# Joining half-unit VectorE products, four Horner halves and a new step order in a sketched-attention and rational-MLP kernel

## The chip, the cores and the metric

The kernel runs on one core of a Trainium2 chip. The metric is the device time of one execution in microseconds (us); the time of a kernel is the median of several executions. The engines are named as in the profile: PE (TensorE, matmuls; PEld is its weight load), DVE (VectorE), ACT (ScalarE), POOL (GpSimd) and SP, whose queue issues nearly all DMAs.

## The reference

```python
def phi(x):                                   # q, k: (4, 4, 1088, 32); S1, S2: (8, 32)
    a = einsum('rd,bhsd->bhsr', S1, x); b = einsum('rd,bhsd->bhsr', S2, x)
    return einsum('bhsi,bhsj->bhsij', a, b).reshape(..., 64)
q_p, k_p = phi(q), phi(k)
kv  = einsum('bhsf,bhsd->bhfd', k_p, v);  z = k_p.sum(axis=2)
x   = einsum('bhsf,bhfd->bhsd', q_p, kv) / (einsum('bhsf,bhf->bhs', q_p, z)[..., None] + 1e-6)
x   = x.transpose(0, 2, 1, 3).reshape(4352, 128)
h   = x @ w_in                                # (4352, 2048)
P   = a0 + a1*h + a2*h*h + a3*h*h*h
Q   = 1 + |b0|*|h| + |b1|*h*h
out = (P / (Q + 1e-6)) @ w_out                # (4352, 128), float32
```

## The kernel before

The first half is a linear attention on sketched features. Keys and values of each of the four batches are loaded whole (`load_k`, `load_v`), transposed on DVE (`kt`), sketched by PE (`ks`, L262), copied by ACT (`kc`), multiplied into 64 features on DVE (`kf`, L274) and summed into kv and z on PE (`kp`, L303); ACT keeps the result (`kk`). Queries go in 13 blocks. For a block, DVE transposes (`qt`, L326), PE sketches (`qs`), ACT copies (`qc`), DVE multiplies (`qf`), PE makes numerator and denominator (`qp`, L366), DVE and ACT divide (`qd`, `qi`, `qx`), PE transposes back (`qb`, L392) and ACT stores the columns in `xT` (`qk`, L399). From block 3 on (class `Spread`), `qc` writes the sketches to DRAM with four DMAs (L421), and three more DMAs read them back with rows repeated, into `a_all` and `b_all` (L424, L427); L433 multiplies these. Each of these tiles has one buffer.

The second half is the MLP, in 17 units. A unit is 4096 columns: so many tokens (256, 512 or, at the end, twice 256) by so many blocks of 128 hidden features. For unit i, PE makes h in four parts of 1024 columns (`h0` to `h3`, L456, in two PSUM tiles `h_ps`), ACT evacuates each as bf16 into `hh` (`e0` to `e3`, L462). DVE computes Q - 1 as (|b1||h| + |b0|)|h| in `u`, `w`, `y` (L485, L491, L496), in one instruction of 4096 columns, or in two halves for the units in `SPLIT_A`. ACT computes r = 1/Q as exp(-ln Q) by halves of 2048 columns (`ln`, L547, and `ex`, L551). The sum a0 r + a1 h r + h h r (a2 + a3 h) is left to PE: `w_out` is held three times, plain and scaled by a0 and by a1. p = a3 h + a2 is made by ACT or DVE (`pa`, L542, or `pd`, L537, by the table `P_ON_ACT`, one entry for each half unit). s = h r is `s` (L555), g = h s is `m` (L559), then g = g p is `x` (L570). `G0` to `G5` (L589) are the matmuls: the blocks of r, s and g of the first half, then of the second.

A Horner half (table `HORNER`, by half unit) goes another way: m makes g = h p, `v` (L565) adds a1, x makes g = g s, and the matmuls on s are left out. So such a half has one DVE instruction more and four or eight matmuls less.

The steps s, m, x and p of a unit are two instructions of 2048 columns, or a single one of 4096 if the unit stands in `WIDE_S`, `WIDE_M`, `WIDE_X`, `WIDE_P` and its halves are of the same kind (both Horner or neither, for m and x; both on the same engine, for p). The tiles r, s and g are rings of four halves, p is a ring of two. Unit 16 is done in a half and two quarters.

The order is written out by hand: `ORDER` is a list of `step:index`, and each engine executes its instructions in that order. Loads are steps too: `lk`, `lv`, `lq` for a batch's keys, values and queries, `lx` for a half of `w_in`, `lw` for a half of `w_out` (cast by `wo`). They all stand in SP's queue with the sketches' DMAs and the stores of the results (`st`, L606, after a DVE transpose, L598). `tn` is a step of idle matmuls on PE (`TURNS`).

```python
    def skip(wide=(), same=None):
        def wrap(f):
            def step(i, h):
                if i in wide and i not in QUARTER and (same is None or same(i, 0) == same(i, 1)):
                    if h != 1:
                        return
                    h = "both"
```

Of the kernel before, what the change touches and what calls it, by code (L numbers as in the profile page):

```python
# [20 lines left out]
ORDER = """
tn:4 tn:0 lw:1 lq:0 kt0:0 lw:0 kt1:0 lx:1 kt2:0 lx:0 ks1:0 kt3:0 ks0:0 lk:1 qt:0 ks2:0 kc0:0 kc1:0 kf0:0 kf1:0 qs:0
kc2:0 qt:1 kf2:0 qc:0 kp0:0 ba:0 kp1:0 qf:0 kp2:0 wo:3 qs:1 kk:0 lv:1 qt:2 qp:0 qc:1 wo:1 qf:1 qs:2 qd:0 qi:0 qc:2
qp:1 qx:0 qf:2 wo:0 qb:0 qp:2 qd:1 qi:1 qk:0 qx:1 qt:3 h3:0 qd:2 qi:2 lq:1 qx:2 wo:4 wo:2 h2:0 e3:0 kt1:1 h0:0 kt0:1
e2:0 pa1:0 u1:0 lk:2 qs:3 w1:0 qb:2 h1:0 y1:0 qc:3 qk:2 e0:0 qt:5 qb:1 ks0:1 qt:4 e1:0 qs:4 qk:1 u0:0 ln1:0 h1:1 qt:6
w0:0 y0:0 kc0:1 ex1:0 h2:1 kf0:1 ks1:1 e1:1 s1:0 e2:1 h0:1 m1:0 kc1:1 ln0:0 kf1:1 h3:1 lq:2 e0:1 x1:0 e3:1 h1:2 kt0:2
ex0:0 u1:1 h2:2 qf:3 w1:1 qc:4 e1:2 qp:3 e2:2 s0:0 pa0:0 h3:2 y1:1 h0:2 qd:3 wo:5 e3:2 qi:3 m0:0 G0:0 e0:2 qx:3 G1:0
ln0:1 kt1:2 x0:0 qb:3 ks0:2 u1:2 qk:3 G2:0 ex0:1 lk:3 pd0:1 G3:0 w1:2 G4:0 pa1:1 kp1:1 y1:2 kc0:2 ln1:1 G5:0 qf:4 lv:2
qs:5 kf0:2 kk:1 ex1:1 qp:4 s0:1 ks1:2 qd:4 qc:5 qi:4 ln0:2 qt:7 G0:1 qx:4 m0:1 qb:4 G1:1 qk:4 s1:1 ex0:2 h3:3 x0:1
kc1:2 h2:3 m1:1 e3:3 kf1:2 h0:3 e2:3 kt1:3 ln1:2 s0:2 h1:3 st:0 m0:2 e0:3 qs:7 x1:1 e1:3 h2:4 ex1:2 u1:3 h3:4 pd1:2  # L30
pa0:2 w1:3 kp1:2 s1:2 e2:4 x0:2 e3:4 h0:4 lv:3 qf:5 pa0:3 y1:3 qp:5 qc:7 e0:4 h1:4 m1:2 qd:5 ln0:3 qi:5 qt:9 G2:1 qx:5
e1:4 x1:2 qb:5 G3:1 qk:5 u1:4 ex0:3 G4:1 m0:3 G5:1 pa1:3 G0:2 w1:4 h0:5 kt0:3 ln1:3 m1:3 h2:5 y1:4 kk:2 ex1:3 ks0:3
G1:2 e0:5 s1:3 G2:2 ln0:4 G3:2 h1:5 v0:3 ex0:4 qf:7 x0:3 G4:2 e2:5 qs:6 s0:4 qc:6 h3:5 e1:5 pd0:4 ln1:4 m0:4 h1:6 v1:3
e3:5 x0:4 pa1:4 h0:6 u1:5 qt:8 G5:2 e1:6 w1:5 ex1:4 h3:6 st:2 y1:5 e0:6 qp:7 e3:6 s1:4 G0:3 pa0:5 lq:3 G2:3 x1:3 qs:8
m1:4 h2:6 ln0:5 m0:5 G3:3 e2:6 x1:4 G5:3 ex0:5 qf:6 G0:4 u1:6 G1:4 qc:8 qd:7 ln1:5 qi:7 qp:6 w1:6 G2:4 qx:7 qd:6 pa0:6
qi:6 v0:5 qb:7 G3:4 qx:6 y1:6 qb:6 qk:7 G4:4 qk:6 ex1:5 h3:7 m0:6 pa1:5 G5:4 s1:5 h1:7 e3:7 st:4 h2:7 m1:5 e1:7 ln0:6
x0:5 h0:7 qt:10 x1:5 e2:7 G0:5 e0:7 qf:8 ks1:3 kc0:3 ex0:6 u1:7 qs:9 h1:8 v0:6 qc:9 w1:7 ln1:6 h3:8 s0:6 e1:8 pd1:6
qp:8 ex1:6 y1:7 h0:8 e3:8 s1:6 kc1:3 ln0:7 h2:8 x0:6 e0:8 m1:6 G2:5 qd:8 ex0:7 G3:5 qi:8 kf0:3 G4:5 kf1:3 G5:5 e2:8
qs:10 ln1:7 u1:8 kp1:3 qx:8 w1:8 ex1:7 qb:8 G0:6 qf:9 qk:8 y1:8 qc:10 h3:9 pa0:7 s0:7 h0:9 e3:9 s1:7 ln0:8 h2:9 qt:12
m0:7 e0:9 G0:7 x1:6 e2:9 h1:10 ex0:8 x0:7 qt:11 h1:9 u1:9 pa0:8 m1:7 G2:6 pd1:7 e1:9 G3:6 s0:8 e1:10 G4:6 u0:9 ln1:8  # L40
h3:10 w1:9 m0:8 qp:9 ex1:8 x1:7 h2:10 x0:8 qd:9 kk:3 e3:10 qi:9 w0:9 pa0:9 h0:10 qf:10 y0:9 qp:10 e2:10 y1:9 e0:10
G5:6 qx:9 qd:10 ln0:9 qi:10 qb:9 s1:8 G1:7 qx:10 G2:7 qk:9 u1:10 ex0:9 G3:7 m1:8 qb:10 G4:7 qk:10 s0:9 ln1:9 G5:7
qs:11 pd1:8 h1:11 w1:10 qc:11 ex1:9 x1:8 h0:11 e1:11 m0:9 pa1:9 h3:11 y1:10 e0:11 G0:8 s1:9 e3:11 h2:11 ln0:10 x0:9
h0:12 m1:9 e2:11 pd0:10 ex0:10 h1:12 u1:11 x1:9 e0:12 G1:8 w1:11 e1:12 G2:8 ln1:10 G3:8 s0:10 G4:8 y1:11 G5:8 ex1:10
qs:12 G0:9 m0:10 G1:9 ln0:11 h3:12 s1:10 ex0:11 x0:10 h2:12 qf:11 pa1:10 m1:10 G2:9 s0:11 G3:9 e3:12 G4:9 x1:10 qc:12
ln1:11 qp:11 pd0:11 m0:11 G5:9 qd:11 e2:12 G0:10 qi:11 x0:11 ex1:11 G1:10 u1:12 G2:10 pa1:11 qx:11 G3:10 w1:12 qb:11
G4:10 qk:11 s1:11 pa0:12 h1:13 y1:12 h3:13 e1:13 m1:11 ln0:12 h2:13 st:6 x1:11 ex0:12 G5:10 qf:12 G0:11 st:8 e3:13
qp:12 s0:12 e2:13 st:10 h0:13 ln1:12 m0:12 u1:13 h2:14 e0:13 x0:12 ex1:12 u0:13 h3:14 w1:13 w0:13 e2:14 y1:13 e3:14
h1:14 pa1:12 y0:13 h0:14 s1:12 qd:12 e1:14 qi:12 m1:12 G1:11 e0:14 qx:12 G2:11 ln1:13 u1:14 qb:12 G3:11 pd0:13 G4:11
ex1:13 w1:14 G5:11 x1:12 G0:12 qk:12 ln0:13 h0:15 s1:13 pd1:13 ex0:13 G1:12 y1:14 G2:12 e0:15 h2:15 s0:13 ln0:14 m1:13  # L50
h3:15 e2:15 m0:13 ex0:14 h1:15 x1:13 x0:13 e3:15 G3:12 s0:14 e1:15 h2:16 ln1:14 u1:15 G4:12 m0:14 ex1:14 G5:12 w1:15
G0:13 h3:16 pa0:14 st:12 y1:15 G1:13 e2:16 G2:13 s1:14 e3:16 h1:16 ln0:15 u2:16 u3:16 w2:16 w3:16 h0:16 x0:14 ex0:15
y2:16 G3:13 pd0:15 e0:16 G4:13 s0:15 e1:16 G5:13 y3:16 pa1:14 G0:15 u0:16 m0:15 G1:15 ln1:15 G0:14 m1:14 G1:14 w0:16
G2:14 ex1:15 x0:15 G3:14 y0:16 G2:15 v1:14 G3:15 ln0:16 s1:15 x1:14 ex0:16 pd1:15 G5:14 m1:15 G0:16 ln2:16 s0:16 G4:15
pa0:16 x1:15 G1:16 ex2:16 m0:16 G5:15 ln3:16 s2:16 x0:16 ex3:16 m2:16 G2:16 pa2:16 st:15 s3:16 G3:16 pa3:16 G4:16
st:14 x2:16 m3:16 G5:16 G6:16 x3:16 G7:16 G8:16 st:16
# [12 lines left out]
@with_exitstack  # L69
def kernel(  # L70
    ctx: ExitStack,
# [409 lines left out]

    @halves(SPLIT_A)
    def d_abs(i, c):
        t = mine(i, "u", mid, 1)
        nc.vector.tensor_scalar(out=t[:, c].bitcast(U16), in0=live[i]["hh"][:, c].bitcast(U16), scalar1=0x7FFF,  # L485
                                scalar2=None, op0=AX.bitwise_and)

    @halves(SPLIT_A)
    def d_w(i, c):
        t = mine(i, "w", mid, 2)  # L490
        nc.vector.tensor_scalar(out=t[:, c], in0=live[i]["u"][:, c], scalar1=ab1, scalar2=ab0, op0=AX.mult, op1=AX.add)  # L491

    @halves(SPLIT_A)
    def d_y(i, c):
        t = live[i]["w"]
        nc.vector.tensor_mul(out=t[:, c], in0=t[:, c], in1=live[i]["u"][:, c])  # L496
# [36 lines left out]

    @skip(WIDE_P, on_act)
    def d_p(i, h, hh):
        if not on_act(i, first(h)):
            nc.vector.tensor_scalar(out=part_of(i, "p", h), in0=hh, scalar1=a3, scalar2=a2, op0=AX.mult, op1=AX.add)  # L537

    @skip(WIDE_P, on_act)
    def a_p(i, h, hh):  # L540
        if on_act(i, first(h)):
            nc.scalar.activation(out=part_of(i, "p", h), in_=hh, func=ACT.Identity, scale=a3_reg, bias=a2)  # L542
# [9 lines left out]

    @skip(WIDE_S)
    def d_s(i, h, hh):
        nc.vector.tensor_mul(out=part_of(i, "s", h), in0=hh, in1=part_of(i, "r", h))  # L555

    @skip(WIDE_M, horner)
    def d_hs(i, h, hh):
        nc.vector.tensor_mul(out=part_of(i, "g", h), in0=hh, in1=part_of(i, "p" if horner(i, first(h)) else "s", h))  # L559
# [6 lines left out]

    @skip(WIDE_X, horner)
    def d_g(i, h, hh):
        g = part_of(i, "g", h)
        nc.vector.tensor_mul(out=g, in0=g, in1=part_of(i, "s" if horner(i, first(h)) else "p", h))  # L570
# [149 lines left out]
```

## Time and profile before

| what | us |
|---|---|
| median of 3 executions (271.52 to 271.73) | 271.63 |
| the profiled execution | 272.05 |
| its span, first to last instruction | 270.3 |
| L456 on PE, 320 records | 125.3 |
| L462 on ACT, 68 | 67.6 |
| L547 and L551 on ACT, 35 each | 66.0 and 65.7 |
| L542 on ACT, 23 | 44.5 |
| L555, L559, L570 on DVE, 33, 30 and 30 in their largest group | 41.1, 35.3, 35.1 |
| L496, L491, L485 on DVE, 22 each | 39.4, 23.8, 21.3 |

The busy times of a line are sums of durations of its records; an f32 matmul has two records. The records of DVE and ACT overlap a little where one instruction follows another at once, so the sum over lines is more than the busy time of an engine. A stretch of the span is read from a table by windows, and single instructions from rows in order of time, which hold start, duration, engine, line, output and inputs.

### The profile page before, as it was taken

To read this page: it belongs to the slowest core of one execution; us is meant where nothing else is said; L and a number is where in the kernel's file an instruction comes from. 1 tells how busy PE (TensorE), PEld (TensorE's weight loads), DVE (VectorE), ACT (ScalarE), POOL (GpSimd) and SP (SyncE) were. 2 spreads that over 40 slices of the span, in tenths; PEclk is the share of its full clock that TensorE was granted. 3 is DMA by queue.
4 is the path that set the end of the run, shared out by engine and by line. 5 is a ranking of instruction groups with operands and counts; after the bars stand their busy time and mean duration, and the time that the engine had idled before them with its cause. 6 is when DMAs were issued, how large, how long until landed. Compare 5 with 4: busy or idle time off the path is not lost.

```text
span 270.3 us, 3749 instructions
## 1 busy us (share of the span) xinstructions
PE 257.8 (95%) x1397; PEld 147.5 (55%) x1397; DVE 256.2 (95%) x278; ACT 247.2 (91%) x224; POOL 2.9 (1%) x24
## 2 busy tenths in 40 slices
...
GB/s 165 281 309 152 148 43 125 124 85 109 63 119 37 12 114 104 76 76 33 97 6 121 9 0 4 118 11 0 18 93 73 44 0 0 2 39 1 0 2 79
DMA packets 30530, 19.55 MB, mean 72 GB/s; under 512 B 20400, under 2 KB 26672, under 8 KB 30512
## 3 DMA queue, kind: packets, MB, share of 16 engines
...
q10 hardware_dynamic: 1648, 0.40, 0.7%
q8 instruction: 11, 0.18, 0.3%
q14 instruction: 7, 0.06, 0.1%
...
## 4 chain that ended last, share of the span: by engine, by line
PE 44%; ACT 25%; DVE 15%; issue 7%; DMA 6%; SPq 1%; DVEq 0%; ACTq 0%
PE h_ps L456 21%; PE att_ps L589 17%; ACT hh L462 8%; ACT ln L547 8%; ACT r L551 6%; DVE s L555 3%; DMA w_in_sb<-in_moe_w_in_dram 3%; DVE w L496 3%; ACT p L542 3%; PE att_ps L366 2%; DVE g L559 2%; DMA q_sb<-in_q_dram 2%; DVE g L570 1%; DVE w L491 1%; DVE k_p L274 1%
## 5 line engine op out<-in xcount | busy, mean ns | idle before, releaser
L456 PE MATMUL h_ps<-xT,w_in_sb 128*128 128x512 f32 (+1 forms) x320 | 125.3, 536 | 2.9 <-ACT hh L462 1.9
L456 PEld LDWEIGHTS h_ps<-xT,w_in_sb 128*128 128x128 f32 x320 | 58.4, 190 | 54.6 <-issue 37.2
L462 ACT CAST hh<-h_ps 128x1024 bf16<-128x1024 f32 x68 | 67.6, 1026 | 4.5 <-PE h_ps L456 4.2
L589 PEld LDWEIGHTS <-w_out 128*128 128x128 bf16 x460 | 45.6, 100 | 45.8 <-issue 14.1
L547 ACT ACTIVATE ln<-w 128x2048 f32<-128x2048 bf16 (+1 forms) x35 | 66.0, 1886 | 0.8 <-DVE w L496 0.7
L551 ACT ACTIVATE r<-ln 128x2048 bf16<-128x2048 f32 (+1 forms) x35 | 65.7, 1878 | 0.6
L542 ACT ACTIVATE p<-hh,a_sb 128x2048 bf16<-128x2048 bf16 (+1 forms) x23 | 44.5, 1940 | 0.2 <-DVE g L570 0.2
L555 DVE TENSOR_TENSOR s<-hh,r 128x2048 bf16<-128x2048 bf16 (+2 forms) x33 | 41.1, 1248 | 0.0
L496 DVE TENSOR_TENSOR w<-w,u 128x4096 bf16<-128x4096 bf16 (+2 forms) x22 | 39.4, 1800 | 0.1
L589 PE MATMUL att_ps<-g,w_out 128*128 128x512 bf16 (+1 forms) x160 | 35.9, 353 | 3.7 <-DVE g L570 3.7
L589 PE MATMUL att_ps<-r,w_out 128*128 128x512 bf16 (+1 forms) x160 | 36.0, 355 | 0.0
L559 DVE TENSOR_TENSOR g<-hh,s 128x2048 bf16<-128x2048 bf16 (+1 forms) x30 | 35.3, 1178 | 0.0
L570 DVE TENSOR_TENSOR g<-g,p 128x2048 bf16<-128x2048 bf16 (+1 forms) x30 | 35.1, 1180 | 0.1
L589 PE MATMUL att_ps<-s,w_out 128*128 128x512 bf16 (+1 forms) x140 | 29.9, 343 | 0.0
L491 DVE TENSOR_SCALAR w<-u,b_abs 128x4096 bf16<-128x4096 bf16 (+2 forms) x22 | 23.8, 1092 | 0.0
L485 DVE TENSOR_SCALAR u<-hh 128x4096 uint16<-128x4096 uint16 (+2 forms) x22 | 21.3, 973 | 0.0
L366 PEld LDWEIGHTS att_ps<-kvz,q_pT 128*128 128x128 f32 x144 | 17.7, 191 | 4.7 <-issue 2.0
L366 PE MATMUL att_ps<-kvz,q_pT 128*128 128x66 f32 x144 | 17.9, 273 | 0.2 <-ACT kvz L315 0.2
L537 DVE TENSOR_SCALAR p<-hh,a_sb 128x2048 bf16<-128x2048 bf16 x12 | 9.7, 810 | 0.0
L303 PEld LDWEIGHTS att_ps<-v_sb,k_p 128*64 128x64 f32 (+1 forms) x288 | 8.8, 138 | 1.7 <-DVE p L537 0.8
L303 PE MATMUL att_ps<-v_sb,k_p 128*64 128x64 f32 (+1 forms) x288 | 9.2, 223 | 0.2 <-DMA v_sb<-in_v_dram 0.2
L255 DVE STREAM_TRANSPOSE kT<-k_sb 128x224 f32<-128x224 f32 (+4 forms) x10 | 5.9, 617 | 3.7 <-DMA k_sb<-in_k_dram 3.7
...
## 6 DMA issues: line engine op xcount, KB each, us to landing
...
```

Source lines behind the costliest of these rows:

```text
L366: nc.tensor.matmul(self.nd[:, o:o + 2 * KW], lhsT=self.q_p[:, c, x:x + 128], rhs=kvz[self.b % 2][:, c, :], start=True, stop=True)
L456: nc.tensor.matmul(t[:, x * tl:(x + 1) * tl], lhsT=w_in_sb[:, f * 128:(f + 1) * 128], rhs=xT[:, x_at(t0):x_at(t0) + tl], start=True, stop= ...
L462: nc.scalar.copy(out=live[i]["hh"][:, part * PW:(part + 1) * PW], in_=live[i]["h", part])
L491: nc.vector.tensor_scalar(out=t[:, c], in0=live[i]["u"][:, c], scalar1=ab1, scalar2=ab0, op0=AX.mult, op1=AX.add)
L496: nc.vector.tensor_mul(out=t[:, c], in0=t[:, c], in1=live[i]["u"][:, c])
L542: nc.scalar.activation(out=part_of(i, "p", h), in_=hh, func=ACT.Identity, scale=a3_reg, bias=a2)
L547: nc.scalar.activation(out=t, in_=live[i]["w"][:, span(h)], func=ACT.Ln, bias=1.0 + 1e-6)
L551: nc.scalar.activation(out=part_of(i, "r", h), in_=live[i]["ln"], func=ACT.Exp, scale=-1.0)
L555: nc.vector.tensor_mul(out=part_of(i, "s", h), in0=hh, in1=part_of(i, "r", h))
L559: nc.vector.tensor_mul(out=part_of(i, "g", h), in0=hh, in1=part_of(i, "p" if horner(i, first(h)) else "s", h))
L570: nc.vector.tensor_mul(out=g, in0=g, in1=part_of(i, "s" if horner(i, first(h)) else "p", h))
L589: nc.tensor.matmul(outs[t0][:, :tl], lhsT=w_sb[y][:, f0 + x, :], rhs=part_of(i, key, h)[:, c:c + tl], start=done[0] == 0, stop=done[0] == ...
```

## The change

Tables and order change, no other code:

- `WIDE_S` goes from 2 units to 15, `WIDE_M` and `WIDE_X` to the same 12, `WIDE_P` from one unit to 8; these steps become one instruction of 4096 columns where the halves are of the same kind.
- `HORNER` has four halves (of units 0, 2, 6 and 9) in place of five (of units 3, 3, 5, 6 and 14).
- `P_ON_ACT` is assigned anew, 23 halves of 34 in place of 22.
- `SPLIT_A` has three units (0, 2, 16) in place of four (0, 9, 13, 16).
- `ORDER` is another order of all steps. At the start, `lx:1` is the first load behind the values, then `lq:0`, `lw:1`, `lk:1`, `lq:1`, `lx:0`, `lw:0`; before, it was `lw:1`, `lq:0`, `lw:0`, `lx:1`, `lx:0`, `lk:1`, `lv:1`, `lq:1`. Two idle matmuls (`tn:4`) go from the beginning to behind the first key sketches. Later loads and blocks have new places too.

```diff
@@ ORDER, from the beginning; all of its lines differ
-tn:4 tn:0 lw:1 lq:0 kt0:0 lw:0 kt1:0 lx:1 kt2:0 lx:0 ks1:0 kt3:0 ks0:0 lk:1 qt:0 ks2:0 kc0:0 kc1:0 kf0:0 kf1:0 qs:0
-kc2:0 qt:1 kf2:0 qc:0 kp0:0 ba:0 kp1:0 qf:0 kp2:0 wo:3 qs:1 kk:0 lv:1 qt:2 qp:0 qc:1 wo:1 qf:1 qs:2 qd:0 qi:0 qc:2
-qp:1 qx:0 qf:2 wo:0 qb:0 qp:2 qd:1 qi:1 qk:0 qx:1 qt:3 h3:0 qd:2 qi:2 lq:1 qx:2 wo:4 wo:2 h2:0 e3:0 kt1:1 h0:0 kt0:1
...
+tn:0 kt0:0 kt1:0 kt3:0 ks1:0 kt2:0 ks0:0 kc0:0 kc1:0 tn:4 qt:0 lx:1 ks2:0 qs:0 lq:0 kf0:0 ba:0 kp0:0 kc2:0 kf1:0 qt:1
+kp1:0 kf2:0 qc:0 qs:1 qf:0 qc:1 qt:2 kp2:0 qt:3 qs:2 qf:1 kk:0 qp:0 qc:2 qf:2 qp:1 qd:0 qs:3 qi:0 qx:0 qb:0 qk:0 qp:2
+qd:2 qd:1 lw:1 h3:0 lk:1 qi:2 qi:1 kt0:1 lq:1 wo:3 h2:0 qx:2 wo:5 qb:2 qt:4 wo:1 qx:1 qt:5 lx:0 qb:1 qs:4 kt1:1 lw:0
...
-P_ON_ACT = (1, 1, 0, 1, 1, 0, 1, 1, 0, 1, 1, 1, 1, 0, 1, 0, 1, 0, 1, 1, 0, 1, 0, 1, 1, 1, 0, 0, 1, 1, 0, 0, 1, 1)
-SPLIT_A = (0, 9, 13, 16)
+P_ON_ACT = (0, 1, 1, 1, 1, 1, 1, 1, 1, 1, 1, 0, 1, 1, 0, 0, 1, 1, 1, 0, 0, 1, 0, 0, 0, 1, 0, 1, 0, 1, 1, 1, 1, 1)
+SPLIT_A = (0, 2, 16)
...
-WIDE_S = (3, 5)
-WIDE_M = (5,)
-WIDE_X = (5, 14)
-WIDE_P = (2,)
-HORNER = (6, 7, 10, 12, 29)
+WIDE_S = (1, 2, 3, 4, 5, 6, 7, 8, 9, 10, 11, 12, 13, 14, 15)
+WIDE_M = (1, 3, 4, 5, 7, 8, 10, 11, 12, 13, 14, 15)
+WIDE_X = (1, 3, 4, 5, 7, 8, 10, 11, 12, 13, 14, 15)
+WIDE_P = (2, 3, 4, 6, 7, 8, 11, 15)
+HORNER = (0, 4, 13, 18)
```

More of the change, by code (lines that the diff above doesn't have):

```diff
@@ L21 @@
 ORDER = """
-tn:4 tn:0 lw:1 lq:0 kt0:0 lw:0 kt1:0 lx:1 kt2:0 lx:0 ks1:0 kt3:0 ks0:0 lk:1 qt:0 ks2:0 kc0:0 kc1:0 kf0:0 kf1:0 qs:0
-kc2:0 qt:1 kf2:0 qc:0 kp0:0 ba:0 kp1:0 qf:0 kp2:0 wo:3 qs:1 kk:0 lv:1 qt:2 qp:0 qc:1 wo:1 qf:1 qs:2 qd:0 qi:0 qc:2
-qp:1 qx:0 qf:2 wo:0 qb:0 qp:2 qd:1 qi:1 qk:0 qx:1 qt:3 h3:0 qd:2 qi:2 lq:1 qx:2 wo:4 wo:2 h2:0 e3:0 kt1:1 h0:0 kt0:1
-e2:0 pa1:0 u1:0 lk:2 qs:3 w1:0 qb:2 h1:0 y1:0 qc:3 qk:2 e0:0 qt:5 qb:1 ks0:1 qt:4 e1:0 qs:4 qk:1 u0:0 ln1:0 h1:1 qt:6
-w0:0 y0:0 kc0:1 ex1:0 h2:1 kf0:1 ks1:1 e1:1 s1:0 e2:1 h0:1 m1:0 kc1:1 ln0:0 kf1:1 h3:1 lq:2 e0:1 x1:0 e3:1 h1:2 kt0:2
@@ L27 @@
[L27 to L56, printed above, removed]
+tn:0 kt0:0 kt1:0 kt3:0 ks1:0 kt2:0 ks0:0 kc0:0 kc1:0 tn:4 qt:0 lx:1 ks2:0 qs:0 lq:0 kf0:0 ba:0 kp0:0 kc2:0 kf1:0 qt:1
@@ new lines @@
+kp1:0 kf2:0 qc:0 qs:1 qf:0 qc:1 qt:2 kp2:0 qt:3 qs:2 qf:1 kk:0 qp:0 qc:2 qf:2 qp:1 qd:0 qs:3 qi:0 qx:0 qb:0 qk:0 qp:2
+qd:2 qd:1 lw:1 h3:0 lk:1 qi:2 qi:1 kt0:1 lq:1 wo:3 h2:0 qx:2 wo:5 qb:2 qt:4 wo:1 qx:1 qt:5 lx:0 qb:1 qs:4 kt1:1 lw:0
+e3:0 qc:3 e2:0 pa1:0 u1:0 qk:2 h0:0 w1:0 e0:0 y1:0 h1:0 ks1:1 qk:1 e1:0 ln1:0 qt:6 ex1:0 h2:1 wo:4 wo:2 pd0:0 u0:0
+w0:0 m0:0 ks0:1 e2:1 kc1:1 h3:1 qs:5 y0:0 s1:0 kc0:1 h0:1 qf:3 kf1:1 lk:2 lv:1 kf0:1 e3:1 ln0:0 kt1:2 h1:1 qp:3 e0:1
+v0:0 qc:4 wo:0 m1:0 e1:1 h1:2 qd:3 ex0:0 qi:3 u1:1 e1:2 h0:2 w1:1 y1:1 kt0:2 qx:3 kp1:1 pa0:1 G3:0 e0:2 h2:2 s0:0
@@ new lines @@
+ln0:1 h3:2 qb:3 x0:0 ex0:1 qf:4 G0:0 lq:2 kk:1 x1:0 qc:5 qp:4 ln1:1 u0:2 qk:3 w0:2 qd:4 e2:2 ks0:2 qi:4 G4:0 kc0:2
+qx:4 y0:2 qb:4 qt:7 G5:0 qs:7 e3:2 qk:4 kf0:2 u1:2 h1:3 w1:2 h2:3 ex1:1 qs:6 s1:1 pa1:1 m1:1 e1:3 qf:5 qc:7 x1:1 e2:3
+h0:3 ln0:2 h3:3 e0:3 qt:9 ex0:2 G2:0 h1:4 e3:3 pa1:2 G0:2 qp:5 y1:2 u1:3 G4:1 w1:3 qd:5 h3:4 G1:1 qt:8 e1:4 y1:3 qf:7
+G0:1 qi:5 lv:2 qc:6 h2:4 ks1:2 lk:3 m0:2 qx:5 v0:2 G3:1 ln1:2 ex1:2 s1:2 e2:4 x0:2 h0:4 ln0:3 e3:4 qb:5 e0:4 m1:2 G5:1
+qk:5 u1:4 G2:1 h3:5 ex0:3 qs:8 kc1:2 x1:2 e3:5 h0:5 w1:4 ln1:3 G5:2 ex1:3 h1:5 kf1:2 qf:6 st:0 e0:5 lq:3 G3:2 y1:4
```

22 lines of the change are left out of this document (added).

## The prediction

> **What bounds the kernel now.** I read the busy times of the engines first, then the same by stage, to see which engine is full where.
>
> ```profile
> PE 257.8 (95%) x1397; PEld 147.5 (55%) x1397; DVE 256.2 (95%) x278; ACT 247.2 (91%) x224; POOL 2.9 (1%) x24
> ```
>
> ```profile
> 0.00:20.00 20.00, 18.07 (x164) 13.26 (x165) 12.94 (x31) 7.17 (x18) 2.94 (x24) 1.00 0.89 251
> 20.00:40.00 20.00, 19.62 (x85) 12.11 (x84) 17.76 (x20) 18.95 (x21) 0.00 (x0) 1.00 0.42 118
> 40.00:60.00 20.00, 19.79 (x187) 14.48 (x187) 19.58 (x21) 19.94 (x21) 0.00 (x0) 1.00 0.40 105
> ...
> 100.00:120.00 20.00, 19.96 (x92) 10.55 (x91) 20.00 (x20) 19.81 (x20) 0.00 (x0) 1.00 0.36 88
> ...
> 220.00:240.00 20.00, 19.80 (x92) 13.20 (x90) 20.00 (x17) 19.94 (x16) 0.00 (x0) 1.00 0.08 13
> ...
> 250.00:260.00 10.00, 7.94 (x50) 5.34 (x49) 10.00 (x11) 9.25 (x7) 0.00 (x0) 0.83 0.01 2
> 260.00:270.30 10.30, 4.83 (x41) 3.70 (x38) 6.17 (x10) 3.85 (x4) 0.00 (x0) 0.91 0.35 52
> ```
>
> The columns are stretch, its length, then busy time of PE, PEld, DVE, ACT and POOL. Three engines are nearly full at once, so a share alone says little. What tells them apart is where each is idle. DVE (VectorE) idles 7.06 us in the first 20, 2.24 in the next 20, 0.42 in the third, and from there it is full in every stretch shown until the tail, where 4.13 us are left over. ACT (ScalarE) idles 12.83 us at the start, and from 250 it has 0.75 and 6.45. PE is full in the middle but has 2.06 and 5.47 us free behind 250, where it waits for DVE. So **DVE sets the end**: 270.3 = 256.2 of work + 14.1 idle, nearly all of it start and tail. ACT and PE follow within a few us. Whatever leaves DVE shortens the kernel until ACT is the next in line.
>
> **What a DVE or ACT instruction costs in a full stretch.** A record's duration overlaps its neighbour's, so I take the time from one start to the next, from the rows in order of time (start, duration, engine, line).
>
> ```profile
> 123.14 1.23 DVE L485 TENSOR_SCALAR u<-hh 128x4096 uint16<-128x4096 uint16 x1
> 124.28 0.75 DVE L565 TENSOR_SCALAR g<-g,a_sb 128x2048 bf16<-128x2048 bf16 x1
> 124.94 1.34 DVE L491 TENSOR_SCALAR w<-u,b_abs 128x4096 bf16<-128x4096 bf16 x1
> 126.20 1.22 DVE L555 TENSOR_TENSOR s<-hh,r 128x2048 bf16<-128x2048 bf16 x1
> 127.33 0.81 DVE L537 TENSOR_SCALAR p<-hh,a_sb 128x2048 bf16<-128x2048 bf16 x1
> 128.06 2.29 DVE L496 TENSOR_TENSOR w<-w,u 128x4096 bf16<-128x4096 bf16 x1
> 130.26 1.23 DVE L555 TENSOR_TENSOR s<-hh,r 128x2048 bf16<-128x2048 bf16 x1
> 131.39 1.23 DVE L570 TENSOR_TENSOR g<-g,s 128x2048 bf16<-128x2048 bf16 x1
> ...
> 245.80 0.69 DVE L485 TENSOR_SCALAR u<-hh 128x2048 uint16<-128x2048 uint16 x1
> 246.40 1.22 DVE L559 TENSOR_TENSOR g<-hh,s 128x2048 bf16<-128x2048 bf16 x1
> ...
> 248.67 0.81 DVE L491 TENSOR_SCALAR w<-u,b_abs 128x2048 bf16<-128x2048 bf16 x1
> 249.39 1.22 DVE L570 TENSOR_TENSOR g<-g,p 128x2048 bf16<-128x2048 bf16 x1
> ```
>
> A product of 2048 columns takes 1.13 us (126.20 to 127.33, 130.26 to 131.39), one of 4096 takes 2.20 (128.06 to 130.26): joining two saves 2 x 1.135 - 2.20 = 0.07. The p of L537 takes 0.73, the addition of L565 0.66, u 1.14 wide and 0.60 narrow, w 1.26 wide and 0.72 narrow.
>
> **DVE, part by part.**
> - s, m, x (L555, L559, L570) become wide in 13, 12 and 12 more units (before, s in two units and m and x in none, since the units named there have one Horner half and one other): 37 joins x 0.07 = 2.6.
> - One unit fewer is split in u, w, y: 0.06 + 0.18 + 0.07 = 0.3.
> - Four Horner halves in place of five: one L565 less, 0.66.
> - p: 12 halves on DVE become 11, 0.73 less, and four of these become two wide instructions. A wide p isn't in the trace; the bounds are no saving and that of the same kind of operation, w, 0.18 each. I take the latter: 0.36, together 1.1.
> - The sum is 4.6, and with the unknown at its bound 4.3; I use **4.5**. It is spread over the whole kernel and DVE is full there, so all of it is on the path.
>
> [...]
>
> **ACT and PE.**
>
> ```profile
> 147.08 1.93 ACT L551 ACTIVATE r<-ln 128x2048 bf16<-128x2048 f32 x1
> 148.90 2.01 ACT L542 ACTIVATE p<-hh,a_sb 128x2048 bf16<-128x2048 bf16 x1
> 150.79 1.93 ACT L462 CAST hh<-h_ps 128x1024 bf16<-128x1024 f32 x2
> 152.59 1.95 ACT L547 ACTIVATE ln<-w 128x2048 f32<-128x2048 bf16 x1
> 154.57 1.91 ACT L551 ACTIVATE r<-ln 128x2048 bf16<-128x2048 f32 x1
> ...
> 261.71 2.17 ACT L542 ACTIVATE p<-hh,a_sb 128x1024 bf16<-128x1024 bf16 x2
> ```
>
> A p on ACT takes 1.89 (148.90 to 150.79). ACT gets one half more, and twelve of its 22 become six wide ones. The wide form isn't in the trace either. Two of 1024 take 2.17 where one of 2048 has a record of 2.01, so a join saves some 0.16; bounds are none and twice that. I take 0.16: +1.9 - 1.0 = **+0.9**, ACT 248.1.
>
> ```profile
> 245.57 1.04 PE L589 MATMUL att_ps<-r,w_out 128*128 128x256 bf16 x8
> 246.45 1.04 PE L589 MATMUL att_ps<-s,w_out 128*128 128x256 bf16 x8
> 247.32 1.03 PE L589 MATMUL att_ps<-r,w_out 128*128 128x512 bf16 x4
> 248.18 1.03 PE L589 MATMUL att_ps<-s,w_out 128*128 128x512 bf16 x4
> ```
>
> A Horner half has no matmuls on s. Units 2, 6 and 9 have one Horner half each and unit 0, which is 256 columns wide, the fourth; before, the five lay in units 3, 3, 5, 6 and 14. So PE gets 8 more matmuls of 512 columns (0.215 each, 247.32 to 248.18 for four) and loses 8 of 256 (0.11 each): **+0.85**, beside the 7.5 us that PE has free behind 250.
>
> **The start.** Loads move in SP's queue: the half of w_in that the first L456 matmuls read goes ahead of all of w_out, the next keys and queries follow, the rest later. On DVE the two casts wo:4 and wo:2 go behind the first u and the transposes qt:4 and qt:5 come ahead of it, about as long, so no net cost.
>
> ```profile
> 21.45 1.01 ACT L462 CAST hh<-h_ps 128x1024 bf16<-128x1024 f32 x1 [0.71 <-PE h_ps L456]
> 21.95 1.37 DVE L255 STREAM_TRANSPOSE kT<-k_sb 128x224 f32<-128x224 f32 x2 [2.48 <-DMA k_sb<-in_k_dram]
> 23.07 0.49 PE L410 MATMUL att_ps<-qT,S 128*64 128x160 f32 x4
> 23.24 0.65 DVE L485 TENSOR_SCALAR u<-hh 128x2048 uint16<-128x2048 uint16 x1
> ```
>
> Now DVE waits 2.48 us for the second keys, transposes them until 23.3, and only then starts u, whose input was ready at 21.45 + 1.01 = 22.46. With keys issued earlier u could start up to 0.75 us sooner. Against it, the sketch of query block 3 (the 0.49 of L410) now stands ahead of the first L456 on PE, and a preceding product waits for a bank. Bounds -0.75 and +0.5; I take 0, because the first L456 is late by about what DVE gains.
>
> **The tail.**
>
> ```profile
> 265.13 0.69 DVE L570 TENSOR_TENSOR g<-g,p 128x1024 bf16<-128x1024 bf16 x1
> 266.51 0.45 DVE L598 STREAM_TRANSPOSE out_sb<-att_ps 128x256 f32<-128x256 f32 x1 [0.69 <-PE att_ps L589]
> ```
>
> From the end of the last product (265.82) to the end of the span are 4.5 us: four matmuls, a transpose and the stores. The new order ends with the same steps, so this stays.
>
> **The sum.** DVE alone: 270.3 - 4.5 = 265.8. ACT alone: 248.1, its start of 12.83 and 1.05 idle, and 5.6 behind its last p (4.5, and two products of 0.57): 267.6 by busy time. But some of ACT's busy time goes when waits go: 147.08 to 148.90 is 1.82 where the input is there, 152.59 to 154.57 is 1.98 where it isn't, so if one in seven of its 224 instructions is such a place, up to 5 us go, and ACT's bound lies between 262.6 and 267.6. Both engines end about equal, and each will sometimes wait for the other: I add 0.7 to DVE's sum and get a span of **266.5**. The execution that was profiled took 272.05, 1.75 more than its span, and the median of the runs is 271.63, 0.42 below it. So 266.5 + 1.75 - 0.42 = **267.8 us**.
>
> **The rivals.**
> - *ACT takes over.* It keeps the 2.8 us of idle that it has between its start and its tail. Then ACT's sum is 267.6 + 2.8 = 270.4 with all of them and 269.0 with half: 270.3 to 271.7 us as a time, 270.3 the likelier. For it: ACT's work rises while DVE's falls, and a wide p holds ACT for some 3.6 us in which no h_ps is evacuated. Against it: most of ACT's waits behind 60 us end with a product of DVE.
> - *The joins are worth the whole record.* 2 x 1.22 - 2.29 = 0.15 each, 3.0 us more off DVE, 262.8; then ACT decides, at the middle of its bounds, 265.1: 266.4 us. For it the records' durations, against it the starts. [...]
> - *The loads still meet the sketches*, so that the reordering doesn't do what it says.
>
> ```profile
> 140.74 1.71 SPq L421 DMA_DIRECT2D sk_d<-sk_sb  x4
> ...
> 149.00:150.00 1.00, 1.00 (x3) 0.29 (x2) 1.00 (x2) 1.00 (x2) 0.00 (x0) 1.00 0.01 3
> ```
>
>   With nothing beside it, a block's sketches go out at 140.74 and are back, sixteen-fold, by 149.0, when the DMA engines fall quiet: 8.3 us. Counting the DVE and ACT work that the new order puts between sk_sb and the product of L433, the tightest blocks get about 12 us. One block that is late by 1 us delays everything behind L433 on DVE: 268.8 us with one, and it takes four to bring back the old time.
> - *Wide means late: slower than before.* A wide x hands both halves of g to PE and frees both halves of p only at its end, 1.1 us after the first half was ready before; p has room for one unit. If ACT's p or PE's L589 is exposed to this once in each of the 12 wide units, that is 13 us against 4.5 won; it decides from five units on. With seven exposed: 7.7 - 4.5 = +3.2, 274.8 us. For it: p's ring is the shortest. Against it: DVE now runs 4.5 us lighter, and the new order has two to four instructions of ACT between x of one unit and p of the next.
>
> **How the numbers follow.** Forecast 0.62 (266.4 to 269.2), ACT takes over 0.16 (269.2 to 271.7), whole records 0.06 (265.2 to 266.4), loads meet sketches 0.06 (268 to 270), late handover 0.10 (over 271.7). 0.2% is 0.54 us, about what a measurement of this kernel can tell from no change: faster means under 271.09, slower over 272.17. Of the ACT case a quarter lies within 0.2%. That gives faster 0.86, same 0.05, slower 0.09. A range from 265.7 to 270.7 holds the forecast, most of the ACT and sketch cases and half of the whole-record case, about 0.82; it covers the start's -0.75 and +0.5 and the price of the wide p on both engines.
>
> **What would show it.** DVE's busy time near 251.7, ACT's near 248, PE's near 258. Wide products start 2.20 apart. DVE idle behind 40 us under 1.5, none of it in front of L433. The first u at 22.5 to 23.5. The last L570 ends at about 262. The forecast is wrong if DVE's busy time falls by 4.5 and its idle time in the middle rises by as much, or if ACT waits at L542 once a unit.

## The result and the profile after

The changed kernel takes **273.76 us** (median of 7 executions, 273.42 to 275.18) and the kernel before 271.68 (7 executions beside them, 271.52 to 271.79). The ratio is 1.0088, 95% interval 1.0067 to 1.011: slower by 2.1 us. The forecast was 267.8, with a range from 265.7 to 270.7. The profiled execution took 274.96; two of the seven lie near 275, the others between 273.4 and 273.8.

First the busy times of the engines, from the page of the changed kernel.

```profile
PE 255.7 (94%) x1381; PEld 148.1 (54%) x1397; DVE 254.1 (93%) x234; ACT 248.3 (91%) x219; POOL 2.9 (1%) x24
```

DVE has 44 instructions fewer and 2.1 us less busy time, ACT 1.1 more. (PE's 1381 matmul records go with 1397 weight loads: 16 records are missing from this trace, so PE's busy time reads a little low.) The prices of the prediction can be read in the changed kernel's rows in order of time.

```profile
58.49 2.29 DVE L557 TENSOR_TENSOR g<-hh,s 128x4096 bf16<-128x4096 bf16 x1
60.70 0.95 DVE L431 TENSOR_TENSOR q_pT<-a_all,b_all 128x768 f32<-128x768 f32 x1
61.56 2.29 DVE L568 TENSOR_TENSOR g<-g,p 128x4096 bf16<-128x4096 bf16 x1
63.77 0.51 DVE L324 STREAM_TRANSPOSE qT<-q_sb 128x320 f32<-128x320 f32 x1
...
64.38 3.79 ACT L540 ACTIVATE p<-hh,a_sb 128x4096 bf16<-128x4096 bf16 x1
67.99 0.25 ACT L375 ACTIVATE den<-att_ps 128x12 f32<-128x12 f32 x1
```

Where DVE doesn't wait, a wide product holds it for 2.21 us (58.49 to 60.70, 61.56 to 63.77), as forecast, and a wide p holds ACT for 3.61 (64.38 to 67.99). So the wide instructions cost what they were said to cost, and the kernel is slower all the same. Where the time went is seen by stage. The stages are the first 40 us, from there to the start of the last evacuation of h (L462, now L460), and the rest, called the tail here; the columns are as in the prediction. First the kernel before, then the changed one.

```profile
0.00:40.00 40.00, 37.69 (x247) 25.36 (x248) 30.70 (x51) 26.12 (x38) 2.94 (x24) 1.00 0.65 185
40.00:244.50 204.50, 201.86 (x1032) 109.75 (x1032) 203.83 (x203) 202.46 (x174) 0.00 (x0) 1.00 0.23 57
244.50:270.30 25.80, 18.28 (x122) 12.36 (x120) 21.67 (x26) 18.57 (x14) 0.00 (x0) 0.90 0.14 21
```

```profile
0.00:40.00 40.00, 37.04 (x253) 25.58 (x254) 29.58 (x53) 25.50 (x38) 2.92 (x24) 1.00 0.64 173
40.00:241.10 201.10, 198.08 (x1001) 109.03 (x1015) 198.45 (x158) 198.85 (x168) 0.00 (x0) 1.00 0.24 59
241.10:273.20 32.10, 20.61 (x130) 13.53 (x130) 26.10 (x25) 23.93 (x15) 0.00 (x0) 0.95 0.17 25
```

The middle is 3.4 us shorter, the tail 6.3 longer. Behind that evacuation the new order leaves DVE 26.1 us of work in place of 21.7 and ACT 23.9 in place of 18.6. It makes h sooner and leaves more of the work on h for later.

Two views of the kernel *before* already spoke against the forecast. The first is who waited for whom between 40 and 240 (engine, line, releaser: us in all, times, longest).

```profile
PEld h_ps L456 <- ACT hh L462: 10.5, 18, 1.5
PEld h_ps L456 <- ACT xT L399: 1.9, 5, 0.9
PE h_ps L456 <- ACT hh L462: 1.9, 4, 0.7
ACT hh L462 <- PE h_ps L456: 0.9, 2, 0.7
PEld att_ps L303 <- DVE p L537: 0.8, 1, 0.8
...
ACT p L542 <- DVE g L570: 0.2, 1, 0.2
```

The second is the chain that ended last.

```profile
PE 44%; ACT 25%; DVE 15%; issue 7%; DMA 6%; SPq 1%; DVEq 0%; ACTq 0%
```

DVE was full, but in this stretch hardly anyone waited for it: 0.8 and 0.2 are the largest rows of PE and ACT that a DVE instruction of the MLP releases. What PE mostly waits for is ACT's evacuation out of the two PSUM tiles of h. (Most of the 10.5 us are waits of the weight load while matmuls run: PE itself idles 2.6 us in the 204.5 of the middle.) The prediction read "full" as "sets the end" and didn't draw on either view.

### The profile page after: what moved, and what is told of

It is laid out like the page before. It is cut to its first block, busy times and chain, and to the rows that moved or that the text cites. A ratio compares the mean times of both kernels' runs of the same rounds, so it can differ in the third digit from the quotient of the medians.

```text
span 273.2 us, 3660 instructions
## 1 busy us (share of the span) xinstructions
PE 255.7 (94%) x1381; PEld 148.1 (54%) x1397; DVE 254.1 (93%) x234; ACT 248.3 (91%) x219; POOL 2.9 (1%) x24
## 4 chain that ended last, share of the span: by engine, by line
PE 56%; DVE 29%; DMA 5%; ACT 4%; issue 3%; SPq 1%; DVEq 0%; ACTq 0%
PE h_ps L454 28%; PE att_ps L587 20%; DVE g L557 5%; DVE g L568 5%; DVE s L553 4%; DMA q_sb<-in_q_dram 4%; DVE w L494 4%; PE att_ps L364 4%; DVE w L489 3%; DVE u L483 3%; PE att_ps L301 2%; ACT hh L460 1%; ACT p L540 1%; PE att_ps L408 1%; PE att_ps L260 1%
## 5 line engine op out<-in xcount | busy, mean ns | idle before, releaser
L454 PE MATMUL h_ps<-xT,w_in_sb 128*128 128x512 f32 (+1 forms) x320 | 127.1, 533 | 1.6 <-ACT hh L460 1.5
L460 ACT CAST hh<-h_ps 128x1024 bf16<-128x1024 f32 x68 | 68.7, 1026 | 1.2 <-PE h_ps L454 1.1
L540 ACT ACTIVATE p<-hh,a_sb 128x2048 bf16<-128x2048 bf16 (+2 forms) x18 | 44.8, 2495 | 0.0
L553 DVE TENSOR_TENSOR s<-hh,r 128x4096 bf16<-128x4096 bf16 (+2 forms) x20 | 39.2, 1960 | 0.0
L587 PE MATMUL att_ps<-g,w_out 128*128 128x512 bf16 (+1 forms) x154 | 34.2, 352 | 2.5 <-DVE g L568 2.1
L587 PE MATMUL att_ps<-r,w_out 128*128 128x512 bf16 (+1 forms) x154 | 34.6, 356 | 1.7 <-ACT r L549 1.4
L557 DVE TENSOR_TENSOR g<-hh,s 128x4096 bf16<-128x4096 bf16 (+2 forms) x19 | 34.9, 1836 | 0.8
L568 DVE TENSOR_TENSOR g<-g,p 128x4096 bf16<-128x4096 bf16 (+2 forms) x19 | 34.8, 1833 | 0.3
L260 PEld LDWEIGHTS att_ps<-S,kT 128*128 128x128 f32 x62 | 7.8, 192 | 3.1 <-issue 1.4
L272 DVE TENSOR_TENSOR k_p<-att_ps,b_sk 128x1280 f32<-128x1280 f32 (+2 forms) x8 | 9.2, 1175 | 0.0
```

The costliest lines, as they stand in the source:

```text
L454: nc.tensor.matmul(t[:, x * tl:(x + 1) * tl], lhsT=w_in_sb[:, f * 128:(f + 1) * 128], rhs=xT[:, x_at(t0):x_at(t0) + tl], start=True, stop= ...
L460: nc.scalar.copy(out=live[i]["hh"][:, part * PW:(part + 1) * PW], in_=live[i]["h", part])
L587: nc.tensor.matmul(outs[t0][:, :tl], lhsT=w_sb[y][:, f0 + x, :], rhs=part_of(i, key, h)[:, c:c + tl], start=done[0] == 0, stop=done[0] == ...
```

## The experiments

All ran beside the kernel before. Eighteen kernels, in the order of the questions; a ratio is to the kernel before, with its 95% interval.

**Do the wide instructions matter?** First the new order with the old tables for s, m and x:

```diff
-WIDE_S = (1, 2, 3, ... 15); WIDE_M = WIDE_X = (1, 3, 4, 5, 7, 8, 10, 11, 12, 13, 14, 15)
+WIDE_S = (3, 5); WIDE_M = (5,); WIDE_X = (5, 14)
 ORDER: s0:i, m0:i, x0:i put in right ahead of s1:i, m1:i, x1:i
```

> The new order with the old WIDE_S, WIDE_M and WIDE_X: each half of s, m and x is an instruction of its own again, the first right ahead of the second. HORNER, P_ON_ACT, SPLIT_A and WIDE_P stay new; nothing is left out. DVE has 2.6 us more of work. ORDER: 275 to 277 us, the joins' gain is lost on top. TABLES: 273 us or less, since halves are handed over earlier.

Measured: 273.83 us (273.37 to 274.69), 1.0083 [1.0065, 1.01]. This is the time of the changed kernel (273.76). The edit undoes 34 of the 37 joins, 2.4 us at 0.07 each, and they are worth nothing here; neither theory's number came. What costs the 2.1 us is not the wide s, m and x. The wide p stayed in, and `HORNER`, `P_ON_ACT`, `SPLIT_A`, `WIDE_P` and `ORDER` were not tried one by one. The counterpart puts the joins into the old order:

```diff
-WIDE_S = (3, 5); WIDE_M = (5,); WIDE_X = (5, 14)
+WIDE_S = (1, 2, 3, ... 15); WIDE_M = WIDE_X = (1, 3, 4, 5, 7, 8, 10, 11, 12, 13, 14, 15)
@@ ORDER, one of the places
-x0:7 qt:11 h1:9 u1:9 pa0:8 m1:7 G2:6 ... m0:8 qp:9 ex1:8 x1:7 h2:10 x0:8 qd:9
+qt:11 h1:9 u1:9 m1:7 x0:7 G2:6 ... qp:9 ex1:8 x1:7 pa0:8 h2:10 qd:9
```

> The old order with the new WIDE_S, WIDE_M and WIDE_X; HORNER, P_ON_ACT, SPLIT_A and WIDE_P stay as before, and only the steps that a wide instruction needs in another place are moved (its halves' inputs ahead of it). Nothing is left out. It has 33 joins of s, m and x: 2.3 us of DVE. Theory ORDER (the new sequence of steps costs the time, the wide instructions are worth their 0.07 us each): 268.8 to 270.5 us, DVE still full from 40 us on. Rival TABLES (a wide instruction takes its inputs late and hands over late, so it costs more in waits than it saves): 272.5 us or more, with DVE or PE waiting at s and x.

Measured: 313.55 us (310.55 to 316.39); the ratio, 1.1499 [1.1444, 1.1553], leaves out the two longest of the six. Contrary to the expectation's words, one thing is left out: in the first halves of units 5 and 6 the addition of a1 stands ahead of the product that it belongs to and is overwritten. Its waits between 40 and 300 are these.

```profile
PEld h_ps L456 <- ACT hh L462: 20.2, 19, 4.5
DVE u L485 <- ACT hh L462: 19.7, 9, 3.5
ACT hh L462 <- PE h_ps L456: 17.2, 12, 6.0
ACT p L542 <- DVE g L570: 12.4, 4, 4.8
```

A wide x frees both halves of p only at its end, and in the old order ACT then stands at p for up to 4.8 us with the next evacuations behind it. This is the mechanism of the rival "wide means late", with 12.4 us of waits where some 42 us were lost (the other waits were not followed to their cause). It is so in a reordering of my own, and not in the changed kernel, where such a wait doesn't occur. So the run shows that the old order can't take the joins as it stands; it doesn't say what the joins are worth in an order made for them.

**Does DVE set the end?** Work was left out on one engine, then on several. In the new order first:

```diff
 d_y:     + if i in (4, 7, 10): return                                  # DVE, L494
 terms:   - ... if y != 1 or not horner(i, n) ...
          + ... if y != 1 or not (horner(i, n) or i in (4, 6, 8, 10)) ...   # PE, L587
 a_p:     - if on_act(i, first(h)):
          + if on_act(i, first(h)) and i not in (4, 8):                 # ACT, L540
```

DVE alone:

> The changed kernel without the instruction y (w times u, 2.20 us) in units 4, 7 and 10: 6.6 us of DVE are left out, and ln reads w itself. PACE: DVE's work is off the path, at most 1.5 us faster than 273.8. LATE: DVE decides, 4 to 6.6 us faster, 267 to 270.

Measured: 273.07 us (272.81 to 274.19), 1.0055 [1.0035, 1.0075]; 0.7 of the 6.6 us come through by the medians. PE alone:

> The changed kernel without the matmuls on s in units 4, 6, 8 and 10 (28 matmuls of 512 columns left out of the result, 6.0 us of PE by 0.215 each). Theory PACE (from 54 to 240 us PE paces the new order and the ACT work behind the last evacuation sets the end): PE reaches its last h earlier, 3 to 5 us faster than the 273.8 of the changed kernel, 269 to 271. Rival LATE (the wide instructions of DVE hand over late, DVE still decides): under 1 us faster, 273.

Measured: 274.15 us (273.36 to 274.81), 1.0080 [1.0051, 1.0109]; nothing. ACT alone:

> The changed kernel without p on ACT in units 4 and 8 (two wide instructions of 3.61, 7.2 us of ACT left out; g is multiplied by an older p). PACE: in the middle ACT follows PE, so 1 to 3 us faster than 273.8 and not 7. LATE: under 1 us. If ACT alone decided: 6 to 7 us.

Measured: 273.38 us (272.41 to 274.49), 1.0057 [1.0027, 1.0087]; 0.4 of 7.2. PE and ACT together:

> The changed kernel with 6.0 us of PE (matmuls on s of units 4, 6, 8, 10) and 7.2 us of ACT (p of units 4 and 8) left out together. Theory TIE (up to the last h, PE, ACT and DVE are each within about 1 us of setting the pace, and in the tail DVE decides): DVE and what is left still hold, 1 to 3 us faster than 273.8. Rival CHAIN (a latency beside the engines sets the pace, the sketches' way through DRAM or the PSUM banks): under 1 us faster.

Measured: 273.26 us (272.84 to 274.16), 1.0063 [1.0044, 1.0083]. All three:

> As before, and y of units 4, 7 and 10 left out too: 6.0 us of PE, 7.2 of ACT, 6.6 of DVE. TIE: 4 to 6 us faster than 273.8, 268 to 270. CHAIN: under 1.5 us faster, over 272.

Measured: 271.98 us (271.46 to 272.94), 1.0016 [0.9994, 1.0037]; 1.8 of at least 6.0. At these doses no engine's work in the middle sets the time by itself. Where PE's dose went is in the waits between 40 and 240, first of the changed kernel, then of the one with PE's dose.

```profile
PEld h_ps L454 <- ACT hh L460: 4.1, 5, 1.4
...
PE h_ps L454 <- ACT hh L460: 1.5, 3, 0.7
```

```profile
PEld h_ps L454 <- ACT hh L460: 11.9, 13, 1.8
PE h_ps L454 <- ACT hh L460: 5.2, 8, 1.1
```

PE reaches the next part of h sooner and waits there for ACT's evacuation. Then the same in the old order, with the forecast's own claim at stake (the edits as above, ACT's in units 5 and 9):

> The old order without the product y (L496) in units 4, 7 and 10: 6.6 us of DVE left out, the wrong Q is used there. If DVE sets the end in the old order, as the prediction has it: 4 to 6.6 us faster than before (265.0 to 267.6). If the time is set by the chain of hand-overs between engines in their fixed order, as the same dose in the new order suggests (0.7 us): 0 to 1.5 us faster.

Measured: 271.61 us (270.8 to 271.89), 0.9992 [0.9982, 1.0003].

> The old order with work left out on all three engines: no s-matmuls in units 4, 6, 8 and 10 (6.0 us of PE), no p on ACT in units 5 and 9 (7.6 us), no y in units 4, 7 and 10 (6.6 us of DVE). If the engines' work sets the old order's time: 5 to 7 us faster than before. If its chain of hand-overs does: 1 to 3 us, as the three together gave 1.8 us in the new order.

Measured: 271.93 us (271.3 to 272.74), 1.0008 [0.9996, 1.0019]. Then DVE's dose four times as large, `if i in range(2, 14): return` in `d_y`:

> The old order without the product y in all of units 2 to 13: 26.4 us of DVE left out, ten times what the change takes off it, nothing from PE and ACT. Theory CHAIN (PE's h parts and ACT's evacuations hold each other through two PSUM tiles, in a fixed order with other work in between, and DVE has to keep up but doesn't set the time): 270.3 to 271.9, DVE waits 20 us more, mostly at u and s for ACT. Rival DVE (it sets the end, the 6.6 us dose fell into a local wait): 267.5 or less.

Measured: 271.47 us (270.83 to 271.9), 0.9992 [0.9982, 1.0001]. **26.4 us less of DVE's work (25.0 by its busy time), and the time stays within 0.2%.** The dose is about six times the 4.5 us of the forecast, not ten times. Its stages and its waits between 40 and 240 (the edit adds two lines, so what stands behind it has numbers higher by 2):

```profile
40.00:244.10 204.10, 201.77 (x1033) 109.98 (x1033) 178.83 (x189) 202.12 (x174) 0.00 (x0) 1.00 0.22 57
244.10:269.90 25.80, 17.06 (x122) 11.69 (x120) 21.65 (x26) 18.55 (x14) 0.00 (x0) 1.00 0.14 22
```

```profile
PEld h_ps L456 <- ACT hh L462: 10.3, 18, 1.3
DVE s L557 <- ACT r L553: 9.6, 6, 2.4
DVE rec L381 <- ACT den L377: 9.5, 6, 2.9
...
DVE u L485 <- ACT hh L462: 4.0, 4, 1.9
```

The last evacuation starts where it did (244.1 and 244.5), PE and ACT are as full as before, and DVE waits 23 us for ACT, at s, at the reciprocal and at u. Last the same omissions on all three engines in twelve units, in the old order and in the new:

> The old order with the same three omissions in all of units 2 to 13: no y (26.4 us of DVE), no p on ACT (15 halves, 28 us), no s-matmuls (20 halves, 17.2 us of PE). Theory JOINT (the three engines are equally full, so work taken from one alone turns into waits for the other two, and work taken from all three at the same places counts): 13 to 17 us faster than before, near PE's dose, the smallest (254.5 to 259). Rival CHAIN (the hand-overs in their fixed order set the time, whatever the work): less than 5 us faster (267 or more).

Measured: 267.38 us (266.59 to 268.1), 0.9827 [0.9806, 0.9848]; 4.4 us, by PE's dose it could have been 17.

> The new order with the same three omissions in units 2 to 13 that took 4.4 us off the old one (no y, 26.4 us of DVE; no p on ACT, 15 halves; no s-matmuls, 21 halves, 18 us of PE). CHAIN: the hand-overs set the time here too, 3 to 7 us faster than after (266.8 to 270.8). Rival: in the new order it is the work, which has become more even; 12 us or more faster (262 or less).

Measured: 264.18 us (263.88 to 264.28), 0.9719 [0.9703, 0.9735], 9.6 under the changed kernel, between the two theories. The waits of the first of the two, between 40 and 240:

```profile
ACT hh L462 <- PE h_ps L456: 20.2, 14, 3.7
PEld h_ps L456 <- ACT hh L462: 12.9, 18, 1.9
DVE s L557 <- ACT r L553: 8.6, 5, 2.9
```

ACT now waits for PE at some evacuations and PE for ACT at others. I read this as an exchange that sets the old order's pace, in which each place has its own slower side, more than the sums of work do. That is argued from the waits: no run gave h a third PSUM tile, and none took work off PE alone or ACT alone in the old order. In the new order about half of the smallest dose comes through.

**Where does the new order lose its time?** Edits at the two ends. At the start, the second queries' load ahead of w_in's first half (`lq:0` and `lx:1` change places):

> The changed kernel with the rest of the queries (lq:0) loaded ahead of the half of w_in (lx:1). The wait of 1.77 us of DVE in front of the transpose at 13.20 goes; the first h comes up to 1.3 us earlier. If the start counts through to the end: 0.8 to 1.5 us faster than 273.8. If the sketches of a later time pace it: no change.

Measured: 273.40 us (273.39 to 273.46), 1.0064 [1.005, 1.0079]. The first evacuation came only 0.2 us earlier (20.79 against 21.00), so this edit tests little. The whole start in the old kernel's places (`kt`, `ks`, `qt`, `kp`, `qp` and so on ahead of `h3:0`):

> The new order with the steps ahead of the first h of unit 0 in the relative places that they have in the old order (the second queries' load and first half of w_in first among the loads); nothing is left out. Theory ENDS (the new order loses its time at its two ends: the first evacuation starts at 21.0 instead of 19.7, and 5.8 us instead of 4.5 lie behind the last product): 272.2 to 272.9. Rival: the late start is made up in the middle, where each engine waits for the others anyway: 273.2 to 273.8, as after.

Measured: 273.61 us (273.34 to 274.58), 1.0075 [1.006, 1.009]. The rows show where the gain ends, first the evacuations of the changed kernel, then with the old start.

```profile
21.00 1.00 ACT L460 CAST hh<-h_ps 128x1024 bf16<-128x1024 f32 x1
...
40.54 1.07 ACT L460 CAST hh<-h_ps 128x1024 bf16<-128x1024 f32 x1
```

```profile
19.90 1.00 ACT L459 CAST hh<-h_ps 128x1024 bf16<-128x1024 f32 x1
...
40.41 1.07 ACT L459 CAST hh<-h_ps 128x1024 bf16<-128x1024 f32 x1
```

Of 1.1 us at the first evacuation 0.13 are left 20 us later: the late start isn't the cause. At the tail, PE's matmuls in another order:

```diff
-... x1:15 G4:15 G1:15 G0:15 ... m0:16 G2:15 G0:16 ... G3:16 ... G5:15 G4:16 ... x3:16 x2:16 G2:16 G8:16 G5:16
+... x1:15 G0:16 G4:15 G1:15 G0:15 ... m0:16 G3:16 G2:15 ... G5:15 G2:16 G4:16 ... x3:16 x2:16 G8:16 G5:16
```

> The new order with three groups of PE's matmuls earlier in the tail: G0 of unit 16 ahead of G4 of unit 15, G3 of 16 ahead of G2 of 15, G2 of 16 right behind G5 of 15; DVE and ACT keep their order, nothing is left out. ENDS: the matmuls fill PE's waits of 2.4 and 2.1 us, 8 to 12 fewer stand behind the last product: 0.8 to 1.6 us faster than after (272.0 to 272.8). Rival: DVE sets the tail, and PE's order there doesn't matter: 273.2 to 273.8.

Measured: 273.75 us (273.33 to 274.07), 1.0073 [1.006, 1.0086]. Both:

> Both of these changes in one kernel. ENDS: the gains add up, 270.9 to 271.8, the time of before or a little under it. Rival: 272.8 or more.

Measured: 273.56 us (273.33 to 274.26), 1.0073 [1.006, 1.0086]. The theory that the loss sits at the very ends has fallen. In all of these the stretch behind the last evacuation keeps its length; here it is with PE's new order.

```profile
40.00:240.80 200.80, 197.78 (x1000) 108.86 (x1014) 198.17 (x157) 198.55 (x168) 0.00 (x0) 1.00 0.24 59
240.80:271.50 30.70, 19.49 (x130) 12.62 (x130) 26.01 (x25) 23.93 (x15) 0.00 (x0) 0.97 0.18 26
```

30.7 us, of which ACT works 23.9; in the kernel before 25.8 and 18.6. What lies beside ACT's work is nearly the same, 6.8 and 7.2 us, and so is what lies beside DVE's (26.0 and 21.7 us of work), 4.7 and 4.1. The length of this tail goes with the order and not with the work in the middle: behind the start of the last evacuation lie 25.7 to 25.9 us in the kernel before and in the four variants of its order that leave work out, whatever the dose, and 30.7 to 30.9 in eight of the variants of the new order. (The variant of the new order with omissions in twelve units has 32.7; three with 32.0 to 32.1 stand at the end of the document.) So the smaller doses in the middle act on the time through the moment of the last evacuation. The chain that ended last in the changed kernel is this.

```profile
PE 56%; DVE 29%; DMA 5%; ACT 4%; issue 3%; SPq 1%; DVEq 0%; ACTq 0%
```

From 233.5 to 259.95 it runs over DVE alone, but for short stretches in which nothing is waited for; in the kernel before it reaches DVE only at 250.5. Two more edits took work from ACT or from DVE in that stretch: p of unit 15 on DVE in place of ACT (`pa1:15` becomes `pd1:15`, two entries of `P_ON_ACT` become 0):

> The changed kernel with p of unit 15 on DVE (1.26 us there) and not on ACT (3.61 us, behind the last evacuation). Nothing is left out. PACE: ACT's work behind the last evacuation counts nearly in full, 1.5 to 3 us faster than 273.8. LATE: DVE has more to do, 0 to 1 us slower.

Measured: 275.21 us (274.83 to 275.43), 1.0124 [1.0104, 1.0145]. And no m in units 14 and 15 (`if i in (14, 15): return` in `d_hs`):

> The changed kernel without m of units 14 and 15 (two wide products, 4.4 us of DVE behind the last h, left out; x multiplies an older g). TIE: DVE decides behind the last h, 2.5 to 4.4 us faster than 273.8, 269.4 to 271.3; the same dose in the middle gave 0.7. CHAIN and any theory with ACT last: under 1 us.

Measured: 274.97 us (273.87 to 275.82), 1.0120 [1.009, 1.0149]. Neither is faster than the changed kernel; the first is slower by its median, the second's executions (273.87 to 275.82) overlap those of the changed kernel. The stretch from 240 on, first of the changed kernel, then with p on DVE, then without the two units' m:

```profile
240.00:275.00 35.00, 21.66 (x135) 14.30 (x135) 27.17 (x27) 25.01 (x17) 0.00 (x0) 0.93 0.15 23
```

```profile
240.00:275.00 35.00, 22.87 (x138) 15.08 (x138) 28.83 (x29) 22.13 (x16) 0.00 (x0) 0.85 0.16 23
```

```profile
240.00:275.00 35.00, 22.70 (x135) 14.80 (x136) 22.95 (x25) 25.03 (x17) 0.00 (x0) 0.86 0.16 23
```

ACT has 2.9 us less to do in the one, DVE 4.2 less in the other, and each time PE's busy time rises by 1 us while its granted clock is lower, 0.85 and 0.86 in place of 0.93. So in the tail, too, relieving one engine doesn't bring the end forward. The rows at the product x of unit 15 show why for DVE's dose, first ACT's p and DVE's x in the changed kernel, then x without the two units' m.

```profile
253.52 3.69 ACT L540 ACTIVATE p<-hh,a_sb 128x4096 bf16<-128x4096 bf16 x1
257.62 2.29 DVE L568 TENSOR_TENSOR g<-g,p 128x4096 bf16<-128x4096 bf16 x1
```

```profile
257.27 2.29 DVE L570 TENSOR_TENSOR g<-g,p 128x4096 bf16<-128x4096 bf16 x1 [2.37 <-ACT p L540]
```

In the changed kernel DVE comes to this product 0.4 us after p is ready. With 4.2 us less of work it comes sooner, but waits for p, and 0.35 us are all that it gains. With p on DVE it is the other way round: DVE, which hardly waits in the tail, has 1.2 us more to do, and ACT waits 4.3 us for it. So at this product, in the tail of the new order, DVE and ACT are within half a microsecond of each other, and both have more to do behind the last evacuation than before. What of the two edits' loss is the lower clock was not tried.

## Why the prediction was wrong, by its steps

- *"DVE sets the end. Whatever leaves DVE shortens the kernel until ACT is the next in line."* **This step failed** for the middle, where the forecast looked for its gain. In the old order 6.6 us off DVE and 26.4 us off it both gave 0.1 us by the medians, with intervals that end at 0.18% (0.5 us), so the 4.5 of the change had next to nothing to give. DVE's full windows meant that its work just fits the pace of the other two, and not that it sets it. DVE's share is 95%, as is PE's, and it could lose 26.4 us for nothing.
- *"ACT's bound lies between 262.6 and 267.6."* This is the same failure seen from the other side. With DVE relieved in units 2 to 13, the kernel still takes 271.5. I let ACT's waits go with DVE's work, on the claim that most of them end with a product of DVE; the waits of before don't show that. Of the rivals, "ACT takes over" (270.3) came nearest to this mechanism; it had ACT keep its idle time, but it didn't have PE and ACT hold each other, and its time was 3.5 us short of the result.
- *The terms of the sum* were right in size: 2.21 for a wide product, 3.61 for a wide p on ACT (two halves 3.78 by the prediction's 1.89, so 0.17 where 0.16 was taken). The first u started at 23.49, inside the 22.5 to 23.5 that was named, and in the changed kernel L433 (now L431) is not among the rows of waits, so the loads did keep off the sketches. DVE's busy time fell by 2.1 and not by 4.5, since it now waits more often (61 gaps between its records in place of 29), and a record that has waited doesn't overlap the one ahead of it (where DVE doesn't wait, the overlap is 0.08 us by the rows of the changed kernel: 58.49 + 2.29 against a start at 60.70). One reading was off: the sketches come back eight-fold (768 KB for 96 that go out) and not sixteen-fold; the 8.3 us don't hang on it.
- *The start: "I take 0".* The first evacuation came 1.3 us later (21.00 against 19.73), which I hadn't seen; but the old start in the new order gave 0.15, so next to nothing of it reached the end.
- *The tail: "this stays".* **This failed too.** I looked only behind the last product, where 4.5 us became 5.0 (5.8 in the profiled execution). What grew most is the stretch behind the last evacuation, from 25.8 to 30.7 us in most kernels with the new order (32.1 in the profiled execution of the changed one), against 3.4 us won in the middle: +1.5, and 2.1 by the medians. That is where the new order's time is lost. The last x ended at 267.4, where the prediction had it at about 262. Neither PE's order in the tail nor less work on DVE or on ACT helped, each alone; both at once was not tried. That the additional work behind the last evacuation is the reason, 5.3 us on ACT and 4.4 on DVE, fits the sums and the rows above and is argued, not shown.
- *Late handover* occurs, as the waits at p with the joins in the old order show, but the changed kernel has an order that avoids it. It was the rival with the nearest time (274.8), by luck, since it is not the cause: without the joins of s, m and x the time is the same.

No version among these that leaves no work out is faster than the kernel before.
